# The column sums of WQ from two rounded products, with a new order of the instructions

## The chip, the cores and the metric

The kernel runs on one core of a Trainium2 chip. The metric is the device time of one execution in microseconds, the median of three runs. TensorE (PE) multiplies, VectorE (DVE), ScalarE (ACT) and GpSimd (POOL) work element by element, and SyncE (SP) issues most of the loads and stores.

## The reference

`x` has 2048 rows of 512 columns in float32. It is normalised by rows, goes through a linear attention with 32 heads and, beside it, through a mixer with an MLP; the two are multiplied and added to `x`.

```python
xn = _layernorm(x, axis=-1)
s = _A_ref(xn, A_wqkv, A_wo)                    # q, k, v = xn @ wqkv; phi; kv, z; num / den; @ wo
g = _silu(_B_ref(xn, B_w1, B_w2, B_w3, B_w4))   # h = gelu(ln(xn) @ w1); shifts; @ w2; MLP w3, w4
return x + s * g
...
phi = lambda t: jnp.where(t > 0, t + 1, jnp.exp(t)) + 1e-6
```

The change touches the very first part: q = xn @ WQ, where WQ is the first 512 columns of `wqkv`. The kernel does not wait for the normalised rows. It multiplies the raw rows by WQ and corrects afterwards: with the row's mean m and its scale r, xn @ WQ = r · (x @ WQ) − r · m · (sum of each column of WQ). So it needs the sum of each of WQ's columns, once. The same is done for k with WK.

## The kernel before, in words

**Products.** Most products are made of three. An operand is split into a rounded part of type fp32r (suffix `h`, written by a ScalarE copy) and the rest (suffix `l`, a VectorE subtraction, original minus rounded part); `rounded` does this. `products` (L495) then issues h·h, h·l and l·h into one PSUM bank. A product marked `slow` (`mm`, L141) is one of full precision: TensorE takes operands of plain float32, and the profile shows it as two records.

**The start of the work.** `Weights` loads a 512x512 weight as four chunks `wk_s` or `wq_s` (a chunk is 128x512), splits each chunk (`wk_0h`, `wk_0l` and so on), and `sums` (L590) adds the four chunks on VectorE with three additions into `wkt` or `wqt`, and multiplies the result by a matrix of ones: `ksum<-wkt,ones` and `qsum<-wqt,ones` on TensorE, whose rows all hold the column sums. `ones` is float32, and `onesr` is the same in fp32r, made at the start and used elsewhere too.

The program lists, in this order: the first four tiles of k (banks `k`; a tile is 128 rows; the transposed input's chunks come as `xt` and are split to `u_0h`, `u_0l` to `u_3h`, `u_3l`; for the first two tiles chunk 0 is multiplied in full precision straight from `wk_s` and `xt`), then `WK.sums` and `wneg`, then `feature_k` of each tile, then WQ's split and `WQ.sums`, then `gram(0)`, `query(0)`, `query(1)` and so on.

`feature_k` (L770) makes phi of k: `kt` on VectorE (needs `wneg`, thus `ksum`), then `kr` and `kt` on ScalarE, `kr` on VectorE, then `k0h` on ScalarE and `k0l` on VectorE. `gram(0)` multiplies `k0h`, `k0l` with the normalised rows `x0h`, `x0l`, so it needs that whole chain. `query` multiplies the `u` parts by the `wq` parts. `qsum` itself is read once, by ScalarE's `qneg`, from which `cq` is made for the queries.

**What sets the order.** Nothing runs in the order of the program text. Every operation is recorded, and `Plan.emit` (L285) is a list scheduler: `deadlines` gives each operation a due time, counted back from the TensorE operation that needs it (TensorE's own due times follow the program's order), `nudged` (L237) then moves the due times of single operations by a table, `SOONER`, of pairs (number of the operation, quarters of a microsecond), and the loop picks for each engine, by a cost for each operation (for a product, L144), the ready operation that is due first. What it picks is issued in that order on each engine, and the engines and SyncE's queue then execute their own lists in order, each instruction waiting for its operands. A list (`in_turn`) fixes the order of the first loads, as far as `x0` and the second halves of `xt`.

Of the kernel before, what the change touches and what calls it, by code (L numbers as in the profile page):

```python
# [411 lines left out]
def linear_attn_gated_by_mixer(  # L412
# [55 lines left out]
    def rounds(name):  # L468

        return piece(name + "h", F32R), piece(name + "l", F32R)  # L470
# [32 lines left out]
    def rounded(hi, lo, full, src=None):  # L503

        pl.act(hi, src or full, AF.Copy)
        split(lo, full, hi)
# [57 lines left out]
    class Weights:  # L564
# [25 lines left out]
        def sums(self, ps):  # L590
            t, r = piece(self.name + "t"), self.raw
            for c in range(1, NC):
                pl.tt(t, t if c > 1 else r[0], r[c], ALU.add)
            pl.mm(ps, ones.all, t, True, True, slow=True)
# [1026 lines left out]
    WQ.sums(qp)  # L1621
# [192 lines left out]
    for b in LINE:  # L1814
# [121 lines left out]
```

## Time and profile before

| | us |
|---|---|
| median of 3 runs | 498.06 (498.03 to 498.6) |
| the profiled execution | 498.08 |
| its span, first to last instruction | 496.4 |
| around the span | 1.7 |
| TensorE busy | 490.6 |
| VectorE, ScalarE, GpSimd busy | 438.4, 373.4, 123.6 |

Times in rows of the trace are microseconds from the start of the span. A row gives start, duration, engine, line, operation, what it writes and reads, shapes, and the number of instructions that the row groups; in brackets stands how long the engine was idle ahead of it and for what. A matmul's duration includes its way through the pipeline, so the time that a product costs is the distance of two starts. The types that a matmul's row shows do not tell the rounded from the full-precision ones; the number of records does.

### The profile page before, as it was taken

The numbers are of one execution on the slowest core, as the hardware profiler recorded it, in microseconds if no ns is written. First come the engines' busy times: TensorE is split into PE (matmuls) and PEld (weight loads), VectorE is DVE, ScalarE is ACT, GpSimd is POOL, SyncE is SP. The second block draws the span as 40 slices with busy tenths as digits, with TensorE's granted clock in tenths as the row PEclk, the third lists the DMA queues.
The fourth block names the chain that finished last, engine by engine and source line by source line (L and its number), as shares of the span: only waits on it lengthen the run. The fifth ranks groups of instructions, "written<-read, shape, count | busy, mean of one in ns | idle before, by whom it ended". The sixth has DMA issues, their size and how long they took to land.

```text
span 496.4 us, 9885 instructions
## 1 busy us (share of the span) xinstructions
PE 490.6 (99%) x3244; PEld 447.0 (90%) x3244; DVE 438.4 (88%) x874; ACT 373.4 (75%) x845; POOL 123.6 (25%) x214
## 2 busy tenths in 40 slices
PE   8999999999999999999999999999999999999996
PEld 6778888888888999899889999999999999999996
DVE  5998997889989669999999999999999899796864
ACT  5999999677887599999988567765686877565531
POOL 1384404276930232133200021100000000143420
PEclk9999999999999999999999999999999999999999
DMA  7869696999974999999988499984634699599996
GB/s 229 303 187 297 133 296 183 237 287 269 329 220 100 236 310 248 273 252 290 337 268 247 158 194 298 247 262 138 183 114 147 215 336 332 114 226 283 278 224 182
DMA packets 87082, 117.44 MB, mean 237 GB/s; under 512 B 10328, under 2 KB 39160, under 8 KB 87032
## 3 DMA queue, kind: packets, MB, share of 16 engines
q1 hardware_dynamic: 75512, 96.11, 59.6%
q0 software_dynamic: 11520, 20.71, 24.9%
q8 instruction: 25, 0.41, 0.4%
q14 instruction: 25, 0.20, 0.1%
HBM read 72.66 MB, written 39.93 MB: 227 GB/s over the span
## 4 chain that ended last, share of the span: by engine, by line
PE 97%; DMA 1%; SPq 1%; ACT 0%; DVE 0%; issue 0%; ACTq 0%
PE pb L146 12%; PE pbd L146 9%; PE h L146 9%; PE g L146 9%; PE acc L146 6%; PE pe L146 6%; PE pbx L146 6%; PE ped L146 5%; PE pbm L146 5%; PE pbs L146 5%; PE q L146 3%; PE pa L146 3%; PE pex L146 3%; PE k L146 3%; PE pad L146 3%; PE pes L146 2%
## 5 line engine op out<-in xcount | busy, mean ns | idle before, releaser
L225 POOL DMA_DIRECT2D xo<-x1d x12 | 10.9, 950 | 166.2 <-DVE xo L191 118.5
L225 POOL DMA_DIRECT2D th<-in_x x14 | 12.2, 895 | 45.0 <-DVE th L201 23.1
L225 POOL DMA_DIRECT2D o<-xnd x16 | 14.0, 887 | 37.5 <-DVE o L191 13.5
L168 ACT ACTIVATE th<-xo 128x512 f32<-128x512 f32 (+1 forms) x16 | 9.7, 614 | 15.9 <-DVE xo L201 10.1
L225 POOL DMA_DIRECT2D zacc<-ke x12 | 12.9, 1073 | 31.4 <-DMA zacc<-ke 10.4
L191 DVE TENSOR_TENSOR ht<-h,abc 128x512 f32<-128x512 f32 x16 | 11.0, 690 | 7.5 <-PE h L146 7.4
L225 POOL DMA_DIRECT2D xt<-nrow x16 | 14.6, 1288 | 8.4 <-ACT k12h L168 4.1
L196 POOL TENSOR_SCALAR w<-mv 128x4 f32<-128x4 f32 (+2 forms) x10 | 2.5, 254 | 40.7 <-ACT sq L168 40.4
L168 ACT ACTIVATE y<-o,nm,rs 128x512 f32<-128x512 f32 x16 | 12.4, 814 | 0.2 <-POOL nm L196 0.2
L168 ACT ACTIVATE p<-pb 128x256 f32<-128x256 f32 x20 | 7.6, 381 | 5.8 <-PE pb L146 5.4
L168 ACT ACTIVATE ht<-ht 128x512 f32<-128x512 f32 x16 | 10.0, 626 | 2.1 <-DVE ht L191 2.0
L168 ACT ACTIVATE sq<-o,mv 128x512 f32<-128x512 f32 x16 | 11.5, 722 | 0.1
L168 ACT ACTIVATE u<-pb 128x256 f32<-128x256 f32 x20 | 7.7, 383 | 5.1 <-PE pb L146 4.5
L201 DVE SCALAR_TENSOR_TENSOR pq<-pq,rd 128x512 f32<-128x512 f32 x16 | 11.0, 688 | 0.3
L168 ACT ACTIVATE p<-pe 128x256 f32<-128x256 f32 x20 | 7.7, 384 | 4.6 <-PE pe L146 4.1
L201 DVE SCALAR_TENSOR_TENSOR qz<-pq,zb 128x512 f32<-128x512 f32 x16 | 10.8, 682 | 0.0
L1471 DVE TENSOR_REDUCE den<-qz 128x32 f32<-128x512 f32 x16 | 10.8, 679 | 0.0
L168 ACT ACTIVATE sq<-o 128x512 f32<-128x512 f32 x16 | 10.0, 629 | 0.1
L613 POOL TENSOR_TENSOR rs<-w,nhalf 128x4 f32<-128x4 f32 (+2 forms) x10 | 9.7, 970 | 0.8
L168 ACT ACTIVATE x<-x,nm,rs 128x512 f32<-128x512 f32 x12 | 9.2, 805 | 0.0
L201 DVE SCALAR_TENSOR_TENSOR th<-th,so 128x512 f32<-128x512 f32 x12 | 8.2, 683 | 0.6 <-ACT th L168 0.5
L168 ACT ACTIVATE sq<-x,mv 128x512 f32<-128x512 f32 x12 | 8.6, 718 | 0.1
(2075 smaller groups left out, 2446.9 us busy)
## 6 DMA issues: line engine op xcount, KB each, us to landing
w_s<-in_w SPq DMA_DIRECT2D x28, 256.0 KB, 5.6
x<-in_x SPq DMA_DIRECT2D x16, 256.0 KB, 6.2
xt<-in_xt SPq DMA_DIRECT2D x16, 256.0 KB, 6.9
xnd<-x SPq DMA_DIRECT2D x16, 256.0 KB, 5.9
xt<-nrow POOLq DMA_DIRECT2D x16, 256.0 KB, 7.6
pqd<-qr SPq DMA_DIRECT2D x16, 256.0 KB, 6.1
o<-xnd POOLq DMA_DIRECT2D x16, 256.0 KB, 6.6
x1d<-o SPq DMA_DIRECT2D x16, 256.0 KB, 5.1
```

Source lines behind the costliest of these rows:

```text
L146: lambda: nc.tensor.matmul(out.get(), lhs.get(), rhs.get(), start=start, stop=stop, skip_group_check=more))
L168: nc.scalar.activation(out.get(), src.get(), func, scale=get(scale), **kw)
L191: self.vec(eng, out, [a, b], lambda: self.e(eng).tensor_tensor(out.get(), a.get(), b.get(), op=op), True)
L196: lambda: self.e(eng).tensor_scalar(out.get(), a.get(), get(s1), get(s2), **kw), False,
L201: lambda: self.nc.vector.scalar_tensor_tensor(out.get(), a.get(), get(s), b.get(), op0=op0, op1=op1),
L225: lambda: self.nc.gpsimd.dma_start(out.get(), get(src), accum_op=ALU.add), mb=mb)
L613: lambda: g.tensor_tensor(out.get(), src.get(), nh.get(), op=ALU.pow))
L1471: pl.add("DVE", .6, .68, [t], [den], lambda: nc.vector.tensor_reduce(den.get(), t.get().rearrange("p (h d) -> p h d", d=DH), axis=AX.X, op ...
```

## The change

`sums` gets a second way, which only WQ uses. The sum of the chunks, `wqt`, is split into a rounded part `wqrh` and a rest `wqrl`, and two fp32r products with `onesr` take the place of the one full-precision product. WK keeps the old way.

The operations' numbers behind it shift by three at most, and the table `SOONER` is a new one throughout.

```diff
-        def sums(self, ps):
+        def sums(self, ps, parts=False):
             t, r = piece(self.name + "t"), self.raw
             for c in range(1, NC):
                 pl.tt(t, t if c > 1 else r[0], r[c], ALU.add)
-            pl.mm(ps, ones.all, t, True, True, slow=True)
+            if not parts:
+                pl.mm(ps, ones.all, t, True, True, slow=True)
+                return
+            ts = rounds(self.name + "r")
+            rounded(*ts, t)
+            for n, v in enumerate(ts):
+                pl.mm(ps, onesr.all, v, n == 0, n == 1)
...
-    WQ.sums(qp)
+    WQ.sums(qp, True)
...
     SOONER = (
-        25, 43, 34, 17, 48, 11, 52, 22, 57, 4, 63, 3, 76, 3, 88, -164, 90, 14, 91, -77, 94, 30, 95, 2, 96, 3,
...
+        15, -86, 28, 6, 39, 37, 40, 17, 46, 28, 56, 87, 65, 26, 76, 3, 88, -109, 91, -73, 104, 45, 105, -34,
...
```

Counted over the whole program, the instructions are the same ones but for the product (one of full precision fewer, two rounded ones more), one ScalarE copy and one VectorE subtraction. The DMAs are the same. The order differs on every engine from the start to the end. Three places of it follow.

VectorE at the start, before, from the first addition of `wk`'s chunks on (`u_1l`, `u_2l` are rests of the input's chunks 1 and 2):

```order
L191 TENSOR_TENSOR wkt<-wk_s_100,wk_s_118 128x512
L191 TENSOR_TENSOR wk_1l<-wk_s_118,wk_1h 128x512
L191 TENSOR_TENSOR wkt<-wkt,wk_s_122 128x512
L191 TENSOR_TENSOR u_1l<-xt_1_120,u_1h 128x256
L191 TENSOR_TENSOR wk_2l<-wk_s_122,wk_2h 128x512
L191 TENSOR_TENSOR wkt<-wkt,wk_s_128 128x512
L191 TENSOR_TENSOR wk_3l<-wk_s_128,wk_3h 128x512
L191 TENSOR_TENSOR u_2l<-xt_2_124,u_2h 128x256
```

The same place now:

```order
L191 TENSOR_TENSOR wk_1l<-wk_s_118,wk_1h 128x512
L191 TENSOR_TENSOR wkt<-wk_s_106,wk_s_118 128x512
L191 TENSOR_TENSOR u_2l<-xt_2_124,u_2h 128x256
L191 TENSOR_TENSOR u_1l<-xt_1_120,u_1h 128x256
L191 TENSOR_TENSOR wk_2l<-wk_s_122,wk_2h 128x512
L191 TENSOR_TENSOR wkt<-wkt,wk_s_122 128x512
L191 TENSOR_TENSOR wk_3l<-wk_s_126,wk_3h 128x512
L191 TENSOR_TENSOR wkt<-wkt,wk_s_126 128x512
```

`u_2l` has moved ahead of `u_1l`, and the second and third addition of `wkt` have moved back, the last one behind `wk_3l`. ScalarE makes `u_2h` ahead of `wk_2h` now, where it was the other way round.

VectorE a little later, before: the last rests of the input, the first tile's `kt`, the additions of `wq`'s chunks, and what follows up to `x0l`.

```order
L191 TENSOR_TENSOR u_1l<-xt_1_120,u_1h 128x256
L201 SCALAR_TENSOR_TENSOR kt_247<-wneg,mv_90,k_116 128x512
L191 TENSOR_TENSOR wqt<-wq_s_169,wq_s_181 128x512
L191 TENSOR_TENSOR wqt<-wqt,wq_s_165 128x512
L191 TENSOR_TENSOR wqt<-wqt,wq_s_186 128x512
L201 SCALAR_TENSOR_TENSOR kr_261<-kt_247,kr_261 128x512
L196 TENSOR_SCALAR x_134<-x_134,rs_92,nm_95 128x512
L191 TENSOR_TENSOR wq_1l<-wq_s_181,wq_1h 128x512
L201 SCALAR_TENSOR_TENSOR k0l<-kr_261,k0h 128x512
L191 TENSOR_TENSOR x0l<-x_134,x0h 128x512
```

The same place now:

```order
L191 TENSOR_TENSOR u_1l<-xt_1_120,u_1h 128x256
L191 TENSOR_TENSOR wqt<-wq_s_160,wq_s_175 128x512
L201 SCALAR_TENSOR_TENSOR kt_251<-wneg,mv_90,k_116 128x512
L191 TENSOR_TENSOR wqt<-wqt,wq_s_181 128x512
L191 TENSOR_TENSOR wqt<-wqt,wq_s_192 128x512
L191 TENSOR_TENSOR u_3l<-xt_3_130,u_3h 128x256
L201 SCALAR_TENSOR_TENSOR kr_262<-kt_251,kr_262 128x512
L196 TENSOR_SCALAR x_133<-x_133,rs_92,nm_95 128x512
L191 TENSOR_TENSOR wqrl<-wqt,wqrh 128x512
L201 SCALAR_TENSOR_TENSOR k0l<-kr_262,k0h 128x512
L191 TENSOR_TENSOR x0l<-x_133,x0h 128x512
```

The first addition of `wqt` has moved ahead of `kt`, `wqrl` stands ahead of `k0l` and `x0l`, and `wq_1l` has moved back: it now comes behind `x0l`, `wq_3l`, `wq_0l`, a statistics instruction and the next tile's `kt`. On ScalarE the new copy `wqrh` stands between `wq_1h` and `k0h`, and `wq_2h` comes behind six squares where it was ahead of `wq_0h`. In SyncE's queue the four loads of `wq` came at places 15 to 18, chunk 2 first, then 0, 1, 3, with a load of `x` behind them; now that load of `x` is ahead, and the four come at places 16 to 19 in the order 0, 1, 2, 3.

TensorE before, from the full-precision product of the second tile's chunk 0 to the sum of WK's columns (`k_116` and `k_167` are the banks of the first two tiles):

```order
L146 MATMUL k_167<-wk_s_100,xt_0_106 128x512
L146 MATMUL k_167<-wk_1h,u_1h 128x512
L146 MATMUL k_167<-wk_1l,u_1h 128x512
L146 MATMUL k_167<-wk_1h,u_1l 128x512
L146 MATMUL k_167<-wk_2h,u_2h 128x512
L146 MATMUL k_116<-wk_1h,u_1h 128x512
L146 MATMUL k_116<-wk_1l,u_1h 128x512
L146 MATMUL k_116<-wk_1h,u_1l 128x512
L146 MATMUL k_116<-wk_2h,u_2h 128x512
L146 MATMUL k_116<-wk_2l,u_2h 128x512
L146 MATMUL ksum<-wkt,ones 128x512
```

The same place now, from chunk 1 on, where the second tile's bank is `k_154`:

```order
L146 MATMUL k_154<-wk_1l,u_1h 128x512
L146 MATMUL k_116<-wk_1h,u_1h 128x512
L146 MATMUL k_116<-wk_1l,u_1h 128x512
L146 MATMUL k_116<-wk_1h,u_1l 128x512
L146 MATMUL k_154<-wk_1h,u_1l 128x512
L146 MATMUL k_116<-wk_2h,u_2h 128x512
L146 MATMUL k_116<-wk_2l,u_2h 128x512
L146 MATMUL k_116<-wk_2h,u_2l 128x512
L146 MATMUL k_154<-wk_2h,u_2h 128x512
L146 MATMUL k_154<-wk_2l,u_2h 128x512
L146 MATMUL k_154<-wk_2h,u_2l 128x512
L146 MATMUL ksum<-wkt,ones 128x512
```

Four products of chunk 1 now stand ahead of the first that reads `u_1l`, where two did, and `ksum` comes three products later than before. The second tile's full-precision product has moved to the front, right behind the first tile's.

133 rows, old and new, of the table SOONER are left out of this document.

## The prediction

> **What bounds the kernel now.** I read the page's busy times first, then the waits of TensorE, then the chain that ended last, then the windows, and then the first 32 us row by row, where the changed sum stands.
>
> ```profile
> PE 490.6 (99%) x3244; PEld 447.0 (90%) x3244; DVE 438.4 (88%) x874; ACT 373.4 (75%) x845; POOL 123.6 (25%) x214
> ```
> ```profile
> PE warm L146 <- POOL ones L529: 1.1, 1, 1.1
> PE k L146 <- DVE u_1l L191: 0.4, 1, 0.4
> ```
> ```profile
> 9.66 1.89 PE k L146 x7
> 11.54 0.86 PE ksum L146 x2
> 12.40 6.27 PE k L146 x27
> 18.67 0.86 PE qsum L146 x2
> ```
> ```profile
> core 0: us, PE busy (x) PEld busy (x) DVE busy (x) ACT busy (x) POOL busy (x), PEclk, DMA share, GB/s
> 0.00:10.00 10.00, 8.58 (x24) 5.82 (x24) 4.11 (x8) 4.96 (x10) 1.33 (x9) 1.00 0.72 217
> 10.00:20.00 10.00, 10.00 (x41) 7.45 (x40) 9.29 (x20) 9.30 (x23) 1.50 (x5) 1.00 0.99 339
> 20.00:30.00 10.00, 10.00 (x44) 8.04 (x44) 9.90 (x22) 9.90 (x21) 7.83 (x17) 1.00 0.51 185
> ...
> 250.00:350.00 100.00, 99.93 (x753) 95.31 (x752) 99.15 (x201) 70.94 (x176) 7.00 (x8) 1.00 0.80 228
> ```
>
> TensorE is busy for 99% of the span, and its list of waits has two entries: 1.1 us at the very start and 0.4 us for `u_1l`. Behind that it runs through to the tail. So a TensorE instruction that goes saves its whole time, and a TensorE instruction that is made to wait adds its whole wait, because nothing behind it has slack to give back. The windows say how near the others are: from 10 to 30 us VectorE is busy 9.29 and 9.90 of each 10 us, ScalarE 9.30 and 9.90. An operand that comes late there has nothing to catch up with.
>
> The chain gives the two prices: 27 rounded products in 6.27 us are 0.232 each, and a full-precision sum is two records in 0.86 us. After a wait the first product takes more: `k` starts at 9.66 behind the wait and the next at 10.00 (the rows below), 0.34 in place of 0.23. I call this 0.11 the restart.
>
> **The product.** One full-precision product of 0.86 goes and two rounded ones of 0.232 come: 0.464 − 0.86 = **−0.39 us**. ScalarE gets a copy to `wqrh` and VectorE a subtraction for `wqrl`. Both are 128x512 and their rows (here `x0h` and `x0l`) show 0.62 and 0.69; in sequence VectorE starts one every 0.60.
>
> ```profile
> 18.33 0.62 ACT L168 ACTIVATE x0h<-x 128x512 fp32r<-128x512 f32 x1
> ```
> ```profile
> 18.73 0.69 DVE L201 SCALAR_TENSOR_TENSOR k0l<-kr,k0h 128x512 fp32r<-128x512 f32 x1
> 19.33 0.69 DVE L191 TENSOR_TENSOR x0l<-x,x0h 128x512 fp32r<-128x512 f32 x1
> ```
>
> The rest of the change is the order. I walked the new order through the first 32 us with the durations of these rows, starting each instruction when its engine and its operands are free, and comparing TensorE at points with equally many products behind them.
>
> **The first wait, `u_1l`.**
>
> ```profile
> 8.50 0.64 ACT L168 ACTIVATE wk_2h<-wk_s 128x512 fp32r<-128x512 f32 x1 [0.74 <-DMA wk_s<-in_wqkv]
> 9.04 0.41 ACT L168 ACTIVATE u_2h<-xt 128x256 fp32r<-128x256 f32 x1
> ```
> ```profile
> 9.18 0.42 DVE L191 TENSOR_TENSOR u_1l<-xt,u_1h 128x256 fp32r<-128x256 f32 x1
> 9.52 0.69 DVE L191 TENSOR_TENSOR wk_2l<-wk_s,wk_2h 128x512 fp32r<-128x512 f32 x1
> 10.12 0.69 DVE L191 TENSOR_TENSOR wkt<-wkt,wk_s 128x512 f32<-128x512 f32 x1
> 10.72 0.69 DVE L191 TENSOR_TENSOR wk_3l<-wk_s,wk_3h 128x512 fp32r<-128x512 f32 x1
> ```
> ```profile
> 9.66 0.51 PE L146 MATMUL k<-wk_1h,u_1l 128*128 128x512 f32 x1 [0.37 <-DVE u_1l L191]
> 10.00 0.40 PE L146 MATMUL k<-wk_2h,u_2h 128*128 128x512 f32 x1
> 10.23 0.40 PE L146 MATMUL k<-wk_1h,u_1h 128*128 128x512 f32 x1
> ```
>
> Now VectorE puts `u_2l` ahead of `u_1l`, and `u_2l` waits for `u_2h` and so for the load of `xt`, chunk 2. That load is issued right behind the one of `wk_2`, which landed at 8.48 (`wk_2h` waited for it to 8.50), and `u_2h` shows no wait at 9.04: it landed between these. I take 8.84, from the times of its transfers: `u_2h` to 9.27, `u_2l` at 9.29, `u_1l` 0.34 later at 9.63 and done at 10.05, TensorE at 10.11. In the new order two more products lie ahead of that wait, so the point to compare is 10.23: −0.12, and the restart gives it back. The step is worth **nothing**, between −0.4 (landed at 8.48) and +0.2 (at 9.04).
>
> **`ksum`.** Behind `u_1l` VectorE now runs `wk_2l`, the second `wkt` addition, `wk_3l`, and the last `wkt` addition, which before stood two places earlier: 9.97, 10.57, 11.17, 11.77, done at 12.46. TensorE leaves 10.11, one restart and seven products later it stands before `ksum` at 10.11 + 0.34 + 7 × 0.232 = 12.08 and waits to 12.52: 0.44 and a restart, **+0.55**. Before, the addition (10.12 + 0.69 = 10.81) was ahead of `ksum` at 11.54 by 0.7; that cover is gone. Bounds: 0.1 if `u_1l` comes early, 0.8 if late.
>
> **`kt` behind `wqt`.**
>
> ```profile
> 13.67 0.74 DVE L201 SCALAR_TENSOR_TENSOR kt<-wneg,mv,k 128x512 f32<-128x512 f32 x1
> 15.01 0.69 DVE L191 TENSOR_TENSOR wqt<-wq_s,wq_s 128x512 f32<-128x512 f32 x1 [0.60 <-DMA wq_s<-in_wqkv]
> 15.74 1.42 DVE L191 TENSOR_TENSOR wqt<-wqt,wq_s 128x512 f32<-128x512 f32 x2
> 17.07 0.68 DVE L201 SCALAR_TENSOR_TENSOR kr<-kt,kr 128x512 f32<-128x512 f32 x1
> ```
> ```profile
> 14.37 0.63 ACT L168 ACTIVATE wq_0h<-wq_s 128x512 fp32r<-128x512 f32 x1 [0.27 <-DMA wq_s<-in_wqkv]
> 14.91 0.71 ACT L168 ACTIVATE kr<-kt,rs 128x512 f32<-128x512 f32 x1
> 15.65 0.73 ACT L168 ACTIVATE kt<-kt,rs 128x512 f32<-128x512 f32 x1
> ```
> ```profile
> 18.51 1.02 PE L146 MATMUL qsum<-wqt,ones 128*128 128x512 f32 x2
> 19.00 0.99 PE L146 MATMUL g<-k0h,x0h 128*128 128x512 f32 x2
> 19.83 0.63 PE L146 MATMUL g<-k0l,x0h 128*128 128x512 f32 x2
> ```
>
> Before, the first tile's `kt` ran at 13.67, in the time in which VectorE would else have waited for `wq` (its row waited 0.60, to 15.01). Now the first `wqt` stands ahead of it. SyncE's queue has a load of `x` ahead of the four of `wq`, whose order is now 0, 1, 2, 3; the two that the addition needs come at the 16th and 17th place of the queue, and the loads in these places landed for the rows at 14.37 and 15.01 before. So `wqt` starts at 15.01 as before, `kt` only at 15.62 (done 16.36). ScalarE's `kr` and `kt` follow at 16.40 and 17.14, VectorE's `kr` at 17.93. The third `wqt` addition (17.00 to 17.69) is followed on ScalarE by `wqrh` at 18.30 behind `wq_1h`, then `k0h` at 18.82 and `x0h` at 19.36 to 19.98; VectorE's `wqrl` waits for `wqrh` and runs from 18.99 to 19.68. TensorE would be at `qsum`'s second half at 19.31 and gets it at 19.73: 0.42 and a restart, **+0.53**, and `x0h` is there in the same moment. So after the product's −0.39 the second pair of gram products stands at 20.54 and not 19.83: +0.7 so far (0.55 − 0.39 + 0.53). Bounds: 0 if the two loads land by 13.7, 1.0 if a load is later by 0.5.
>
> VectorE takes its instructions strictly in their order in this trace (`wqt` waits at 15.01 with `kr` and others behind it). [...] By that rule `kt` cannot pass the waiting `wqt`, which is the +0.53; if it could, that term would be 0.
>
> **The first queries.** VectorE is 1.5 us behind its old times here and never idle, so what it makes last is late next: `wq_1l`, which before was ready at 18.82, now stands behind `wqrl`, `k0l`, `x0l`, `wq_3l`, `wq_0l`, a `BN_STATS` and the next `kt`.
>
> ```profile
> 23.10 0.39 PE L146 MATMUL q<-wq_1l,u_1h 128*128 128x512 f32 x1
> ```
>
> Six instructions of 0.60 and one of 0.65 from 18.99 put it at 23.25 to 23.94. TensorE comes at 23.10 + 0.7 = 23.8: 0.2 and a restart, **+0.3** (0 to 0.5). `wq_2l` fits within 0.1 and gets no term.
>
> **The row averages.** GpSimd's chain (`pu`, `an`) feeds a transposition on TensorE.
>
> ```profile
> 27.69 1.01 POOL L613 TENSOR_TENSOR an<-pu,nhalf 128x4 f32<-128x4 f32 x1
> ```
> ```profile
> 30.79 0.27 PE L151 MATMUL ab<-ident,an 128*8 128x128 f32 x1
> ```
>
> `an` was ready at 28.70, 2.1 before it was needed. Two squares on ScalarE and the moments on VectorE that it needs come later now; my walk ends it at 32.05, with TensorE there at 31.7: **+0.4** (0 to 0.8).
>
> **The sum.** −0.39 + 0.55 + 0.53 + 0.3 + 0.4 = +1.4. Behind 36 us every engine has another order, of the same work; the old order held without a wait of TensorE, and I take 0 for the new one, with 0 to +1.0 as the bounds, since VectorE's 99.15 busy of 100 us from 250 to 350 leaves a late operand no room. The profiled execution took 498.08 us (span 496.4 and 1.7 around it); the median of the runs is 498.06, so they are the same. 498.08 + 1.4 = **499.5 us**.
>
> **Rivals.**
> - *Only the product shows.* The loads of `wq` land by 13.7, when VectorE is through with `u_1l`, and the input's load by 8.5, so that `wqt`, `kt` and the last `wkt` are where TensorE needs them. For it: between 8.50 and 14.37 the 16th load took its time, and nothing in the order makes it so. Against it: the loads ahead are the same ones, in almost the same order. It decides at 13.7 us. Time 498.08 − 0.39 = 497.7, and with the old wait for `u_1l` (0.37 and its restart) gone too, 497.2.
> - *One of the two big waits.* `ksum`'s or `qsum`'s alone: 498.08 − 0.39 + 0.54 = 498.2, with the wait for `wq_1l` or `an` up to 499.0.
> - *More waits behind 36 us.* VectorE, without slack from 250 to 350 us, delays an operand there, or a weight's load comes late in the new order: one to two waits of 0.5 on top of the forecast, 500.2 to 501.
> - *The waits cost more than their length.* [...] No wait worked out here is above 0.45, and behind the trace's own wait of 0.37 the next product took 0.34 and the one behind it 0.23. It gets no chance.
>
> **How the numbers follow.** The forecast has 0.38, only the product 0.24, one of the two waits 0.20, more waits 0.18. About 0.2%, 1.0 us, is what a measurement of this kernel can tell from no change: 497.06 to 499.06 is "the same". The forecast lies above that but for 0.04; half of the rival of the product alone (0.12) may fall below it, if the start gains on top of its two terms. Slower: 0.34 + 0.18 = 0.52; the same: 0.04 + 0.12 + 0.20 = 0.36; faster: 0.12. The range goes from 497.2 to 500.7: it leaves out what is below the product alone with the first wait gone and the upper half of the last rival.
>
> **What would show it.** Right: TensorE's waits list `ksum` for `wkt` (0.4), `qsum` for `wqrl` (0.4), `q` for `wq_1l` (0.2), and VectorE's `wqt` shows a wait for `wq_s` of over 1 us with `kt` behind it near 15.6. The product: `qsum` two records of 0.23. Wrong: `wqt` starting before 14 us, `ksum` without a wait, or TensorE's first gram product at 19 us. A wait of TensorE behind 36 us would be the third rival.

## The result, and the profile after

The changed kernel takes **503.73 us** (median of 4 runs, 502.97 to 504.54) beside 498.04 (497.94 to 498.6) of the kernel before: a ratio of 1.0112, interval 1.0091 to 1.0133. It is slower, by 5.7 us. The forecast was 499.5 and its range ended at 500.7.

The profiled execution is the slowest of the four, 504.54 with a span of 502.4, so 6.5 above the profiled execution before. Its busy times, the waits of TensorE (us in total, times, longest) and the window from 10 to 20 us:

```profile
PE 493.7 (98%) x3244; PEld 448.0 (89%) x3244; DVE 438.5 (87%) x875; ACT 373.5 (74%) x846; POOL 128.2 (26%) x214
```
```profile
PE pem L146 <- ACT p5m L168: 1.8, 1, 1.8
PE warm L146 <- POOL ones L529: 1.0, 1, 1.0
PE pb L146 <- DVE h_a220f L191: 0.6, 1, 0.6
PE q L146 <- DVE kt L201: 0.3, 1, 0.3
PE ksum L146 <- DVE wkt L191: 0.3, 1, 0.3
PE k L146 <- DVE u_1l L191: 0.3, 1, 0.3
...
```
```profile
10.00:20.00 10.00, 9.68 (x38) 6.91 (x39) 8.75 (x17) 8.54 (x21) 2.71 (x5) 1.00 1.01 358
```

VectorE and ScalarE do 0.1 us more than before; what grew is TensorE's time. Its list had one wait behind the warm-up and has six now (the last, not shown, is 0.2 for a load), and in the window TensorE stands idle 0.32 us where it was busy throughout. The largest wait, 1.8 us, is no place that the change names: it is the mixer's product `pem` at 186 us. TensorE's busy time grew as well (490.6 to 493.7) though it executes less; the microseconds behind that wait show where 1.7 of the 3.1 come from (the third column from the end is the granted clock):

```profile
185.00:186.00 1.00, 0.00 (x0) 0.00 (x0) 0.00 (x0) 1.00 (x4) 0.19 (x1) 1.00 1.06 410
186.00:187.00 1.00, 0.98 (x8) 0.98 (x9) 0.21 (x1) 1.00 (x3) 0.94 (x1) 1.00 0.86 328
187.00:188.00 1.00, 1.00 (x7) 1.00 (x7) 0.91 (x2) 1.00 (x3) 0.83 (x3) 0.52 0.55 211
188.00:189.00 1.00, 1.00 (x7) 1.00 (x7) 0.69 (x2) 1.00 (x3) 0.36 (x1) 0.50 0.99 373
189.00:190.00 1.00, 1.00 (x6) 1.00 (x6) 0.12 (x1) 0.97 (x2) 0.00 (x0) 0.50 0.17 49
190.00:191.00 1.00, 1.00 (x9) 1.00 (x8) 1.00 (x3) 0.39 (x1) 0.00 (x0) 0.77 0.00 0
```

For 3.4 us TensorE runs at half its clock: 0.48 + 0.50 + 0.50 + 0.23 = 1.71 us are lost in it.

**Where the time went.** I compared TensorE in the two traces at the points behind which the same products lie. There the changed kernel is 1.0 us behind at 34 us (what the product saves is in it), 1.2 at 184, 4.8 at 192, 5.0 at 301, 6.2 at 310 and 6.3 at the end. So the start costs 1.0, the place at 184 us 3.6 (the wait of 1.76, 1.71 by the clock and a restart) and the place near 303 us 1.2. The other 0.4 are steps of 0.2 and less that I cannot place. The span grew by 6.0.

*The start*, in TensorE's rows:

```profile
12.30 1.13 PE L146 MATMUL ksum<-wkt,ones 128*128 128x512 f32 x2 [0.28 <-DVE wkt L191]
...
18.81 0.39 PE L146 MATMUL qsum<-wqrh,onesr 128*128 128x512 f32 x1
19.25 0.49 PE L146 MATMUL qsum<-wqrl,onesr 128*128 128x512 f32 x1
...
20.12 0.63 PE L146 MATMUL g<-k0l,x0h 128*128 128x512 f32 x2
...
22.91 0.51 PE L146 MATMUL q<-wq_0h,u_0h 128*128 128x512 f32 x1 [0.30 <-DVE kt L201]
```

The sum's two records take 0.44 and 0.33 from start to start, where 0.23 is the usual distance: 0.2 more for `wqrl` and a restart. The second gram pair is at 20.12, where it was at 19.83.

*The middle.* ScalarE and TensorE at 184 us:

```profile
184.13 0.63 ACT L168 ACTIVATE sq<-o 128x512 f32<-128x512 f32 x1 [2.29 <-DMA o<-xnd]
...
184.88 0.72 ACT L168 ACTIVATE sq<-o,mv 128x512 f32<-128x512 f32 x1
...
185.60 0.36 ACT L168 ACTIVATE p5m<-pem 128x256 f32<-128x256 f32 x1
```
```profile
186.02 0.38 PE L146 MATMUL pem<-w_b22h,hs41h 128*128 128x256 f32 x1 [1.76 <-ACT p5m L168]
```

`p5m` copies a PSUM bank out and so frees it for the next `pem`. It needs nothing but that bank, but in ScalarE's list two squares of `o` stand ahead of it now, and the first of these waits 2.29 us for a gather, `o<-xnd`. GpSimd issued that gather at 175.78 (before 174.50); TensorE was 1.2 us behind there already, so this is the same point of its work:

```profile
175.78 0.86 POOL L225 DMA_DIRECT2D o<-xnd  x1 [2.94 <-ACT o L168]
```

It landed 8.27 us on, at 184.05, where it took 7.41 before:

```profile
175.78 8.27 DMA o<-xnd
```

Before, the copy stood ahead of the squares, and they came at 182.00, right behind the gather's landing at 181.91:

```profile
174.50 0.86 POOL L225 DMA_DIRECT2D o<-xnd  x1 [2.88 <-PE h L146]
...
181.48 0.39 ACT L168 ACTIVATE p5m<-pem 128x256 f32<-128x256 f32 x1
182.00 0.63 ACT L168 ACTIVATE sq<-o 128x512 f32<-128x512 f32 x1
```

*Near 303 us.* TensorE fills a bank with six products of `yt31`, the last from 302.64 on, and needs it emptied for `yt41` at once:

```profile
302.64 0.28 PE L146 MATMUL pb<-yt31h,w_s1l 128*128 128x256 f32 x1
303.56 0.38 PE L146 MATMUL pb<-yt41h,w_b 128*128 128x256 f32 x1 [0.65 <-DVE h_a220f L191]
```

VectorE's `h_a220f`, which empties it, starts at 303.10. Before, six products `pb<-yt21` stood between the two:

```profile
297.66 0.28 PE L146 MATMUL pb<-yt31h,w_s1l 128*128 128x256 f32 x1
297.77 0.30 PE L146 MATMUL pb<-yt21h,w_s0h 128*128 128x256 f32 x1
...
298.50 0.34 PE L146 MATMUL pb<-yt41h,w_b 128*128 128x256 f32 x1
```

From 302.64 to 303.56 are 0.92 in place of 0.12: 0.8 us for a place in a list, and 0.1 for the restart. The next `yt41`, at 308.90, comes 0.3 late in the same way.

### The profile page after: what moved, and what is told of

Read it like the earlier page. It is cut to its first block, busy times and chain, and to the rows that moved or that the text cites. A ratio compares the mean times of both kernels' runs of the same rounds, so it can differ in the third digit from the quotient of the medians.

```text
span 502.4 us, 9899 instructions
## 1 busy us (share of the span) xinstructions
PE 493.7 (98%) x3244; PEld 448.0 (89%) x3244; DVE 438.5 (87%) x875; ACT 373.5 (74%) x846; POOL 128.2 (26%) x214
## 4 chain that ended last, share of the span: by engine, by line
PE 85%; DVE 6%; DMA 6%; issue 1%; SPq 1%; ACT 1%; DVEq 0%; ACTq 0%
PE pb L146 11%; PE pbd L146 9%; PE g L146 8%; PE h L146 7%; PE pbx L146 6%; PE pe L146 5%; PE ped L146 5%; PE pbs L146 4%; PE acc L146 4%; PE pbm L146 4%; DMA o<-xnd 3%; PE q L146 3%; PE pex L146 3%; PE pa L146 3%; PE pad L146 3%; PE pes L146 2%
## 5 line engine op out<-in xcount | busy, mean ns | idle before, releaser
L201 DVE SCALAR_TENSOR_TENSOR xo<-pbd,p5d 128x256 f32<-128x256 f32 x6 | 2.5, 424 | 7.1 <-PE pbd L146 7.1
```

The lines of the kernel that those rows point to most:

```text
L201: lambda: self.nc.vector.scalar_tensor_tensor(out.get(), a.get(), get(s), b.get(), op0=op0, op1=op1),
```

## The experiments

The change does two things at once, so there are two theories. **Order**: the new list holds the loss, at a few places or all along. **Sum**: the new way of summing holds it. In the experiments the scheduler's choice is replaced by a written order and written buffers, so that one kernel's list can run with single instructions moved. All times are medians, and each ratio is to the kernel before in the same group of runs (there 498.2 to 498.65).

### Which half holds it: e1, e2

e2 is the new order with the old sum:

```diff
-    WQ.sums(qp, True)
+    WQ.sums(qp)
```

> The new order, with the full-precision product back in its place and wqrh, wqrl left out. Theory 'order': 503 to 504.5 us, TensorE waits about 1.8 us for p5m near 184 us and 0.6 us for h_a220f near 303 us as in the changed kernel. Theory 'sum': 498 to 499.5 us, these two waits gone.

Measured: 503.2 us (502.55 to 504.1), 1.0098 [1.0081, 1.0115]. The loss is all there without the new sum: in its trace every engine's list is the changed kernel's but for the sum. Its waits:

```profile
PE pem L146 <- ACT p5m L168: 1.4, 1, 1.4
PE k L146 <- DVE u_1l L191: 1.3, 1, 1.3
...
PE pb L146 <- DVE h_a220f L191: 0.7, 1, 0.7
PE ksum L146 <- DVE wkt L191: 0.3, 1, 0.3
```

The waits at 186 and 303 us are the changed kernel's. Behind the 1.4 the clock does not halve: its mean over this trace is 0.999, over the changed kernel's 0.995. The product alone (e2 against the changed kernel, 1.0098 and 1.0112) makes no difference that these intervals tell.

e1 is the old order with the new sum, with some instructions moved to make room (a `cq` of ScalarE also moves, behind `k1h`):

```diff
 ScalarE
 wq_1h
+wqrh
 k0h
 x0h
+sq        (of the next tile, from further ahead)
 VectorE
+wqrl
 k0l
 x0l
+wq_1l     (from ahead of k0l)
 ...
 x1l
+x         (the third tile's, from 3 us ahead)
```

> The order of before, written out instruction by instruction, with the new sum put into it: wqrh behind wq_1h on ScalarE, wqrl ahead of k0l on VectorE, the two products at the old place; four instructions with slack (wq_1l, a square, a cq, the third tile's x) step back to make room. Theory 'order' (the loss is in the new order of ScalarE's, VectorE's and TensorE's lists, not in the sum): 497.5 to 498.4 us, no wait of TensorE above 0.3 us behind 20 us. Theory 'sum' (the copy and the subtraction, in engines that are 99% busy from 20 to 30 us, push everything behind them late): 500 us or more, with waits at 28 us and later.

Measured: 500.63 us (500.03 to 502.27), 1.0050 [1.0031, 1.0070]. More than I gave the sum, and at a place that I had not thought of:

```profile
43.80 0.50 PE L146 MATMUL q<-wq_0h,u_0h 128*128 128x512 f32 x1 [1.80 <-ACT u_0h L168]
```

The row averages' store `nrow<-ar` left at 32.88 (before 31.39), so the gathers of the second block's `xt` and their split `u_0h` came late, and the clock fell behind that wait too, to 0.50 from 44.44 to 47.86.

### The old order with the new sum: e10, e15, e17, e8, e11

e10 moves the copy `ar` ahead of `k2h` on ScalarE.

> The old order with the new sum, as in e1, but on ScalarE the row averages' copy ar ahead of k2h, behind which it stood. Theory that e1's 2.4 us came from ar, the store of nrow and the gathers of xt that follow it: the wait for u_0h of 1.8 at 43.8 us and the low clock behind it are gone, 498.3 us (498.0 to 498.8). Rival, that the store is late because of the transfers ahead of it in the queue and not because of ar: the wait for u_0h stays above 1 us, 499.5 to 500.8.

Measured: 500.95 us (499.61 to 502.49), 1.0052 [1.0036, 1.0067]. The rival came out: `ar` was early, and the store left at 32.81, as late as in e1, behind stores of `x` in SyncE's queue of which one waited for the third tile's normalised rows. That instruction was the one I had moved myself in e1. e15 puts it back:

```diff
 VectorE
+x         (the third tile's, at its old place)
 ...
 x1l
-x
```

> The old order with the new sum, as in e10 (ar ahead of k2h), and the third tile's normalisation back at its old place on VectorE, so that the stores of x ahead of the row averages' store in SyncE's queue are not late. Theory that e1's loss came from that queue: the wait for u_0h is gone, 498.3 us (497.9 to 498.9). Rival, that the 0.6 us which the copy and the subtraction take from ScalarE and VectorE come back at the row averages in any case: 499.3 to 500.8 with a wait for u_0h of over 0.5 us.

Measured: 499.51 us (498.76 to 500.04), 1.0020 [1.0011, 1.0029]. The wait for `u_0h` is gone (the store is issued at 32.19), so 1.1 of e1's loss was my edit's (with `ar` moved as in e10, which by itself had brought nothing). What is left, 1.4 us in this execution, begins with its waits:

```profile
PE k L146 <- DVE u_1l L191: 0.7, 1, 0.7
PE qsum L146 <- DVE wqrl L191: 0.4, 1, 0.4
PE g L146 <- ACT k2h L168: 0.2, 1, 0.2
```

`u_1l` is a matter of when the loads land in an execution: e4 below has the lists of before there and waits 1.3 for it. A product's duration covers 0.16 us of a delay (its row shows 0.39, and the next one starts 0.23 behind it), which the list leaves out, so the costs come from the points with equal products: with their restarts 0.1 for `u_1l`, 0.6 for `wqrl`, of which the product gives 0.39 back, 0.4 at 23.05 ahead of the product of `wq_0l` (too short for the list), 0.5 for `k2h` and 0.2 at 43 us. e17 takes the wait for `wqrl` away by doing the sum later:

```diff
 ScalarE
-wqrh
 k0h
 x0h
+wqrh
 VectorE
-wqrl
 k0l
 x0l
+wq_0l
+kt        (the second tile's)
+wq_1l
+wqrl
 TensorE
-qsum<-wqrh
-qsum<-wqrl
 g         (the first block of k)
 q x6
+qsum<-wqrh
+qsum<-wqrl
```

> As e15, the old order with the new sum, but wqrh behind x0h, wqrl behind wq_0l, the second kt and wq_1l, and the two products of qsum behind six products of the first queries. Theory that e15's loss is the two waits of the sum (0.37 and about 0.2 with their restarts): 499.5 less 0.8 is 498.7 us (498.2 to 499.0), and the product's 0.39 goes for VectorE's 0.6 later on (k2h waited for). Rival, that nothing is left to lose and the 0.39 is earned: 498.2 or less. Second rival, that the wait only moves on: 499.3 or more.

Measured: 499.88 us (499.65 to 500.56), 1.0034 [1.0021, 1.0047]; the second rival. The wait came back as one for `x0h` (the profiled execution, the slowest, loses another 0.8 at 311 us, where TensorE waits for ScalarE's `p`):

```profile
19.20 0.73 PE L146 MATMUL g<-k0h,x0h 128*128 128x512 f32 x2 [0.72 <-ACT x0h L168]
```

This row says more than the time. `x0h` was done at 19.15 here (18.54 + 0.61) and at 18.95 before (18.33 + 0.62), so without a sum at that place TensorE stands idle until then: the k products were through at 18.51 before. Of the old product's 0.86 some 0.4 lay where TensorE would have waited for `x0h` anyway. The product was cover.

e8 leaves the copy and the subtraction to GpSimd, which in the kernel before is busy for 0.10 of the 6 us from 14 to 20:

```diff
-            rounded(*ts, t)
+            (GpSimd) wqrh <- wqt
+            (GpSimd) wqrl <- wqt - wqrh
```

with `kr` and `x0` ahead of the last `wqt` on VectorE, `wq_1l` behind `x0l`, and `qsum` behind the first gram products.

> Before's order with the new sum and its rounding on GpSimd (idle from 14 to 20 us): ScalarE and VectorE run what they ran before, with kr and x0 ahead of the last wqt addition, wq_1l and one square a little later, and qsum's two products behind gram(0). If the cost of the old-order run (500.6) came from the two instructions on ScalarE and VectorE, it is gone: 497.5 to 498.0 us, the product's 0.39 us saved. [...]

Measured: 499.27 us (498.79 to 500.92, 12 runs), 1.0017 [1.0008, 1.0027]. GpSimd's subtraction runs from 19.18 for 1.62, and beside it VectorE is slow:

```profile
18.54 1.10 DVE L191 TENSOR_TENSOR x0l<-x,x0h 128x512 fp32r<-128x512 f32 x1
19.56 1.78 DVE L191 TENSOR_TENSOR wq_1l<-wq_s,wq_1h 128x512 fp32r<-128x512 f32 x1
```

These two take 0.69 each in the kernel before, so beside GpSimd VectorE loses 1.5 us (0.41 and 1.09), more than the 0.6 that it saves; TensorE waits 0.69 for `wq_0l`. e11 moves `wq_0l` ahead of the second `kt`.

> The old order with the rounding and the rest made on GpSimd, as in e8, but on VectorE wq_0l ahead of the second tile's kt and the statistics that stood ahead of it. Theory that e8's wait of 0.7 for wq_0l is its whole loss and that the product's 0.39 is earned: 499.3 less 0.8 is 498.5, about the kernel before, down to 497.9 if the wait is not replaced. Rival, that VectorE is short there by what GpSimd takes from it (1.5 us over x0l and wq_1l), so that the wait comes back at kt, wq_1l or wq_2l: 499.0 to 499.5.

Measured: 499.68 us (498.96 to 501.34, 9 runs), 1.0024 [1.0013, 1.0034]: the rival; TensorE now waits 0.3 for that `kt`. So of six ways to run the new sum in the old order none is as fast as the old sum; the best two lose 0.9 us.

### The place at 184 us: e3, e4, e5, e12, e13, e16

e3 changes one thing in the changed kernel; e4 goes the other way in the kernel before and puts `p5m` behind the two squares:

```diff
 ScalarE, e3
+p5m<-pem
+u2m<-pbm
 sq<-o
 sq<-o,mv
-p5m<-pem
-u2m<-pbm
```

> The changed kernel, with the two squares of ScalarE that wait for the fourth tile's o<-xnd transfer moved behind p5m and u2m. Theory 'queue' (p5m stood behind a square that waited for a DMA): the wait of 1.8 us at 184 us is gone and with it the dip of the granted clock from 185 to 190 us: 1.8 to 3.3 us less, 500.4 to 502.0 us. Rival 'transfer' (the late transfer holds TensorE by another way, through the statistics or the rows that follow): the wait comes back within 10 us, 503 us or more.

> Before, with the one thing turned round: the same two squares moved ahead of p5m on ScalarE, nothing else. Theory 'queue': TensorE waits for p5m near 183 us for 1.0 to 1.5 us, 499.1 to 499.8 us if a wait costs its own length, and 500 to 501.5 us if TensorE's granted clock falls behind it as in the changed kernel's profile (from 185 to 190 us it was 0.70). Rival 'transfer': no wait above 0.3 us, 498.0 to 498.4 us.

e3: 502.87 us (502.13 to 502.91), 1.0087 [1.0072, 1.0102]. `p5m` is no longer waited for, and the wait is back 2.6 us later, for the next user of the late gather's chain:

```profile
188.65 0.39 PE L146 MATMUL pbm<-w_t4h,ha221h 128*128 128x256 f32 x1 [1.60 <-DVE o L191]
```

VectorE's `o` stood behind `w_1l`, which waited for ScalarE's `w_1h`, which stood behind the squares. The clock stays at 1.00.

e4: 499.51 us (498.83 to 500.31, 7 runs), 1.0022 [1.0011, 1.0033]. The order of these few rows alone costs the kernel before 1.1 us, and its trace has the same wait:

```profile
184.78 0.39 PE L146 MATMUL pem<-w_b22h,hs41h 128*128 128x256 f32 x1 [1.32 <-ACT p5m L168]
```

So a copy that stands behind the two squares costs TensorE a wait, in either order. But the squares of e4 did not wait for this gather: it had landed at 180.10, and ScalarE, which the gather before it had held up for 0.73 until 176.14, was busy from there on.

```profile
182.90 0.62 ACT L168 ACTIVATE sq<-o 128x512 f32<-128x512 f32 x1
...
183.65 0.72 ACT L168 ACTIVATE sq<-o,mv 128x512 f32<-128x512 f32 x1
...
184.37 0.36 ACT L168 ACTIVATE p5m<-pem 128x256 f32<-128x256 f32 x1
```

At 182.90, ahead of the squares, the copy would have been done at 183.26, before TensorE came for the bank at 183.46; the squares put it 1.47 us later. That the late gather holds the copy in the changed kernel is read from its trace; no run has its order with an early gather. The price of this place in the changed kernel I tried to take out as a whole, four times: e5 and e12 put `o` ahead of `w_1l` as well (e12 also `wo_2h` and `wo_3h` behind the four `y`), e13 puts `p1m`, `kvrh` and `p5m` ahead of these two and, at 174 us, the copy that the gather's issue waits for ahead of a square; e16 also `o` and `wo_1h`:

```diff
 ScalarE, e16
 ...
 y x3
+p1m
 y
 kvrh
 p5m
+o
+wo_1h
+wo_2h
 ha112h
 u2m
 ha122h
+wo_3h
```

> The changed kernel with the middle spot freed: the two squares that wait for the transfer behind p5m and u2m on ScalarE as in the run before, and on VectorE o<-pbm,p5m ahead of w_1l and wo_2l (its buffer exchanged with wo_3h's, so that it needs no buffer of theirs). Theory 'queue' (in the run before, TensorE's wait moved from p5m to o, because o stood behind w_1l, which stood behind w_1h and the squares): no wait of TensorE above 0.3 us from 180 to 200 us, granted clock 1.00 there, and 500.8 to 501.7 us. Rival 'transfer': a wait of over 1 us remains between 180 and 200 us, 502.5 us or more.

> The changed kernel with the place at 184 us alone set right: p5m and u2m ahead of the two squares, the addition o ahead of w_1l, wo_2h and wo_3h behind the four y. Theory that the wait and the low clock behind it hold 3 us: 503.7 less 3.0 is 500.7 (500.2 to 501.3), clock 1.00 from 184 to 200 us. Rival, that only the low clock of 1.6 us is to be had since the wait comes back behind: 502 to 503, as in e3.

> The changed kernel with the place at 184 us alone set right: on ScalarE the addition's copy o ahead of a square that it stood behind, p5m and u2m ahead of the two squares of the fourth o, p1m, kvrh and p5m of the next pair ahead of wo_2h and wo_3h; on VectorE o ahead of w_1l. Theory that the wait of 1.8 and the low clock behind it hold 3 us: 500.7 us (500.2 to 501.5), clock 1.00 from 184 to 200 us, no wait above 0.7 behind 36 us. Rival, that the late gather of o only moves the wait on to the y and what hangs on them: 502 or more, with a wait of over 1 us between 186 and 205 us.

> As e13, the changed kernel with the place at 184 us alone set right, and besides on ScalarE p5m, o and wo_1h of the next pair ahead of wo_2h, and wo_3h behind two of the splits of ht. Theory that the wait of 1.8 with the low clock behind it holds 3 us: 500.7 us (500.2 to 501.8), no wait above 0.7 between 180 and 205 us, the lag of TensorE behind the kernel before about the same at 205 us as at 180. Rival, that the late gather moves the wait on whatever stands in front: 502.5 or more, a wait of over 1 us there again.

| | us | ratio | waits of TensorE between 180 and 205 us |
|---|---|---|---|
| e5 | 504.07 | 1.0108 [1.0092, 1.0124] | 1.0 for `kvt` |
| e12 | 504.98 | 1.0128 [1.0115, 1.0141] | 2.3 for `p1m`, then half the clock |
| e13 | 505.16 | 1.0138 [1.0124, 1.0152] | 1.7 for `o` |
| e16 | 503.99 | 1.0111 [1.0095, 1.0127] | 0.7 for `u2m`, 0.6 for `o` |

The wait came back each time. `p5m` is on time in all four, and another instruction of ScalarE or VectorE that stood behind something late takes its place; in e12 it was `p1m` behind `wo_3h`, which waited for a buffer, so my own edit. In e16's trace TensorE still loses 1.8 us there, and in e2's, with this place as the change has it and the clock at 1.00, 1.7: the mends gained nothing but the clock. That this place can be had for nothing with the gather landing at 184 us is not shown.

### The start and 303 us: e6, e7, e9, e14

e6 sets the start right by the prediction's steps (`u_1l` ahead of `u_2l`, the last `wkt` ahead of `wk_3l`, `kt` ahead of the first `wqt`), e7 also the middle of e5 and the six products at 303 us:

```diff
 TensorE, e7
 yt31 x6
+yb111 x6
 yt41 x6
-yb111 x6
```

> The changed kernel with only its start put right: u_1l ahead of u_2l, the last wkt addition ahead of wk_3l, the first tile's kt ahead of the wqt additions and its kr ahead of the last of them, k0h and x0h ahead of wqrh, qsum's two products behind gram(0). The reasons of the prediction: the waits for wkt, wqrl and kt go, 0.8 to 1.3 us less than the changed kernel, 502.0 to 503.0 us. Rival: a slower start gives the later stages slack, so that an earlier TensorE waits there longer, and the time stays within 0.4 us of 503.2.

> The changed kernel with the start and the middle spot put right as in the two kernels beside it, and at 303 us six products of another bank (yb111) ahead of the six (yt41) that waited for h_a220f. Theory 'queues' (three spots hold the whole loss): 498.2 to 499.6 us. Rival 'order throughout' (the new order is slower in many small places): 500 us or more.

e6: 503.98 us, 1.0108 [1.0089, 1.0126], with a new wait of 1.1 for `k0l`: my edit had left `wqrl` ahead of `k0l` while its `wqrh` went behind `x0h`. e7: 504.41, 1.0115 [1.0094, 1.0135]; the wait for `h_a220f` is gone and one of 0.5 for `h_a120f` stands behind it. e9 and e14 mend both edits and do all three places again, e9 with the middle of e12, e14 with that of e13.

> The changed kernel, with three places set right and all else in its new order: at the start u_1l ahead of u_2l, kt ahead of the first wqt, the last wkt addition ahead of wk_3l, wqrh and wqrl behind x0h and x0l, then wq_0l, the second kt, wq_1l and wq_2l; at 184 us p5m and u2m ahead of the two squares, the addition o ahead of w_1l, wo_2h and wo_3h behind the four y; near 303 us the six yb111 products ahead of yt41. Theory that these three places hold the loss: 503.7 less 3.0 (the middle with its low clock), 0.7 (303 us) and 0.9 (the start) is 499.1 us, 498.5 to 500, no wait of TensorE above 0.5 but warm. Rival, that the new order is short of room in many places and a wait that is taken away comes back somewhere behind: 501 or more, with a wait of 0.5 or more in another place, as in the two earlier attempts at it.

> As the kernel with the middle set right, and besides the six yb111 products ahead of yt41 near 303 us, and at the start u_1l ahead of u_2l, kt ahead of the first wqt, the last wkt addition ahead of wk_3l, wqrh and wqrl behind x0h and x0l, then the second kt, wq_0l, wq_1l. Theory that three places hold the loss: 500.7 less 0.7 and less 0.8 is 499.2 us (498.6 to 500). Rival, that the new order has no room at other places either: 500.5 or more, with waits of 0.5 and more elsewhere.

e9: 507.54, 1.0179 [1.0164, 1.0194], two waits of 2.3, one of them for a `kt` that I had put behind `wq_2l`. e14: 504.62, 1.0126 [1.0112, 1.0140]: no wait for `ksum`, `qsum` or `kt`, but 0.5 for `x0h`, 0.3 for `wk_2h` and 0.2 for `wk_2l`; the 1.7 of e13; 0.5 for `h_a120f`, and TensorE still falls back by 1.2 between 301 and 310 us. So what the place at 303 us costs is read from the trace, and no run took it out. No set of mends that I found brought the changed kernel below e3's 502.87, which its interval does not tell from the changed kernel.

## Why the prediction was wrong

1. **Order, not product, decides**: right in kind. The forecast was slower than before for reasons of order, and e2 shows that the order holds the loss.
2. **The start, +1.4**: right in kind, 1.0 in the trace. `u_1l` was −0.2 (nothing said) and `ksum` +0.54 with its restart (+0.55). The sum was nothing (+0.14 said, 0.53 less the product's 0.39), because `wq` landed at 14.47 and not at 15.01. The first queries were +0.6 (0.3), but for a bank that the second tile's `kt` had to free and not for `wq_1l`, and the row averages +0.2 (0.4). That the sum of the terms came near is in part luck: three of them missed by 0.2 to 0.3, in both directions. The load for `wqt` did come first in VectorE's list and did hold `kt` back behind it (1.22 of waiting, then `kt` at 15.08), as said.
3. **The step that failed**: "Behind 36 us every engine has another order, of the same work; … and I take 0 for the new one, with 0 to +1.0 as the bounds". It was 5.2 in the profiled execution: 3.6 at 184 us, 1.2 at 303 to 309 and the small steps. The rival of more waits behind 36 us was right in kind, with a chance of 0.18 and a price of 0.5 a wait. The price was taken from the waits of the start, where an operand is late by a fraction of an instruction. At 184 us a copy stood behind two squares, which alone take 1.47 us of ScalarE, and in the changed kernel the first of these waited 2.29 for a gather. The orders of 184 and 303 us could be read ahead of the run: squares ahead of `p5m`, `yt41` directly behind `yt31`. I compared the first 36 us only.
4. **"The waits cost more than their length … It gets no chance."** Wrong: in the profiled execution 1.7 us of the 3.6 are the low clock (1.71 by the granted clock; e2, whose trace has the same wait, 1.41 long, at full clock, loses 1.7 there in all). It is not in every execution: the mean clock of this one is 0.995, of the three others 0.999, at 502.97 to 504.28, so the loss of the median is nearly all waits.
5. **"A TensorE instruction that goes saves its whole time"**: wrong at this place. e17 shows that some 0.4 of the product's 0.86 lay over TensorE's wait for `x0h`, and e8 and e15 that its 0.39 is not earned even in the old order: 0.6 each on ScalarE and VectorE, busy 9.3 to 9.9 of 10 us there, come back as waits (in e15 0.4 ahead of the product of `wq_0l` and 0.5 for `k2h`).

What stays open: why the gather at 175 us takes longer in the new order. It lands 8.1 to 8.8 us behind its issue in all eleven traces of the new order, and 4.6 to 7.4 in the eight of the old one. In each of the eleven SyncE issues the store `x1d<-o` and the load of `wo_s` 0.9 to 2.1 us ahead of it; in each of the eight that load comes 2.1 to 3.0 us behind it. No run moves these two, so that they hold the gather up is not shown. Nor is it known whether the new order can be mended at 184 us at all.

## What to carry to other kernels

In a kernel whose first engine is busy 99%, read a new order to its end before pricing it: look in each engine's list for copies that free a bank and stand behind an instruction with a DMA among its operands, and for a bank that is refilled directly behind its last product. Before counting a removed instruction as gain, remove it in the trace by hand: when its successor's operands are not there earlier, it was cover. An order that holds many tight places may not be mended one place at a time by hand; here four attempts at one place each made a new wait. And the list of waits is not the whole loss: compare the starts at points behind which the same products lie.

## What the runs showed of the hardware

**The clock.** Whether a wait of TensorE lowers its clock does not go by its length alone. In e9 there are two of 2.29 us:

```profile
24.00:25.00 1.00, 0.42 (x1) 0.11 (x1) 1.00 (x2) 0.97 (x2) 0.84 (x3) 1.00 0.00 0
25.00:26.00 1.00, 0.00 (x0) 0.00 (x0) 0.97 (x4) 0.72 (x2) 0.92 (x4) 1.00 0.00 0
26.00:27.00 1.00, 0.29 (x1) 0.29 (x2) 1.00 (x2) 0.25 (x1) 0.84 (x4) 1.00 0.04 8
27.00:28.00 1.00, 1.00 (x6) 0.79 (x6) 1.00 (x3) 1.00 (x2) 0.65 (x1) 1.00 0.08 16
...
196.00:197.00 1.00, 1.00 (x8) 1.00 (x8) 1.00 (x2) 1.00 (x5) 0.20 (x1) 0.73 1.03 375
197.00:198.00 1.00, 1.00 (x6) 0.90 (x5) 0.67 (x3) 1.00 (x4) 0.67 (x1) 0.50 0.94 256
198.00:199.00 1.00, 1.00 (x7) 1.00 (x6) 0.85 (x3) 0.12 (x1) 0.53 (x1) 0.50 1.05 272
199.00:200.00 1.00, 1.00 (x5) 0.86 (x5) 0.60 (x2) 0.51 (x1) 0.34 (x1) 0.56 0.98 227
```

Behind the first, which ends at 26.71, the clock stays full; behind the second, which ends at 195.49, it halves from 196.46 on for 3.41 us (0.27 + 0.50 + 0.50 + 0.44 = 1.71 lost). It halved behind waits of 1.76 (the changed kernel), 1.80 (e1) and 2.29 (e12), and not behind 1.41 (e2), 1.60 (e3), 1.72 (e14) and 1.73 (e13); and at the start of e13 and e11, behind two waits of 0.6 to 0.95 within 3.1 us, it halved as well. In each of these six falls (the changed kernel, e1, e9, e11, e12, e13) the granted clock adds up to 1.71 us lost.

The times at which the clock changes go with this. In the traces of the two kernels they lie whole multiples of 3.413 us apart: the changed kernel's record of the full clock begins at 6.14, the clock falls at 187.04 (53 × 3.413 later), rises at 190.46 and falls at 501.07 (91 × 3.413 later), behind the last product; in the kernel before the record begins at 7.00 and the clock falls at 495.11 (143 × 3.413 later), behind the last product too. An estimate from these numbers: a trace is cut into steps of 3.413 us, counted from its fall. Then the first wait of e9 is parted at 25.79, 50 steps ahead of the fall, into 1.37 and 0.92, and the second lies whole between 193.04 and 196.46. The steps that end in a fall between products have 1.55 (e13 and e11), 1.77 (the changed kernel), 1.80 (e1) and twice 2.29 us (e9, e12) of waiting in them. The later wait of e13, 1.73 us long, is parted at 195.32 into 1.16 and 0.57, and the clock stays full behind it; in the two kernels' traces no other step between the start of the record and the last product has more than 0.53. (e3 and e14 show no fall between products to count from.) So in these traces the falls go with TensorE's waiting within one step. No run moves a wait across the end of a step, so that this is the cause is not shown.

**GpSimd beside VectorE.** In e8 a 128x512 subtraction on GpSimd took 1.62 us, and VectorE's subtraction of the same size beside it 1.78, where it takes 0.69 in the kernel before. Both slow instructions of VectorE there, this and `x0l` (1.10 in place of 0.69), ended 0.54 to 0.55 us behind the GpSimd instruction that they overlap (a cast to 19.09, the subtraction to 20.80).
